# In-projection weights, block rows, query load and mask products of a block-sparse attention kernel with a gated MLP

## The chip, the cores and the metric

The kernel runs on one core of a Trainium2 chip. The time is the device time of one execution in microseconds; the kernel before has a median of 218.33 us over 3 runs (215.74 to 220.37). A profile is one further execution, recorded instruction by instruction. Its engines: PE (matmuls and transposes; PEld are its weight loads), DVE (vector), ACT (activations), POOL (GpSimd), SP (here only the issue of DMAs; SPq in the profile).

## The reference

Four sequences of 768 positions, 8 heads of 64. Attention is limited to blocks of 32 positions: the neighbours, the first and last block row and column, and three sampled blocks for each row of blocks. The result goes through a gated MLP whose gate mixes positions.

```python
scores = scale * np.matmul(q, k.transpose(0, 1, 3, 2))
mask = np.abs(blk_i - blk_j) <= window
mask = mask | (blk_i == 0) | (blk_j == 0) | (blk_i == n_blocks - 1) | (blk_j == n_blocks - 1)
for qb in range(n_blocks):
    for kb in sampled_blocks[qb]:
        mask[qb * block:(qb + 1) * block, kb * block:(kb + 1) * block] = True
scores = np.where(mask, scores, -1000000000.0)
...
attn = attn / (np.sum(attn, axis=-1, keepdims=True) + 1e-09)
x = matmul(attn, v)                       # heads side by side: 768 x 512
h = np.maximum(x @ w_in, 0.0)             # 512 x 1024
u, v = h[..., :512], h[..., 512:]
v_n = (v - mu) / np.sqrt(var + 1e-06)
v_s = np.einsum('ts,bsd->btd', w_spatial, v_n) + b_spatial[None, :, None]
out = (u * v_s) @ w_out
```

## The kernel before

**The mask inside the product.** The tile `kq` has 88 rows (`KR`): rows 0 to 63 hold the transposed keys and queries of a head (keys in columns `K_`, queries behind them; `qcols(t, n)` are the n query thirds of 256 columns from third t), rows 64 to 87 (`MR`) hold the mask. In the key columns they are a one-hot row of the block that a key belongs to; in the query columns they are -300 for each block that the query may not see, and 0 elsewhere. So one matmul over 88 rows gives scores with the mask added. The table `bm` (24 blocks x 24 blocks) is worked out on DVE from iotas and from `samp`, the sampled blocks; `mask_rows` (L293) multiplies it with the one-hot rows on PE and copies the product of one query third into the rows `MR` of head 0. `rows` (L249) copies those rows from head 0 to other heads.

**The first sequence** is done in units (`UNITS`), each of two heads by a third of the queries (pair 0: one head by two thirds), with three slots per unit, 36 slots in all. In each slot `qk_unit` multiplies queries with keys into a PSUM tile (`ps`, tag sc, two of them), and ACT takes the exponential (L438, 128 x 1024). Three to five slots later `av_unit` multiplies with the values, and DVE normalises (L461, L462). Slots 0 to 5 are pair 0, slots 6 to 14 the first query third of pairs 1 to 3, slots 15 to 23 the second third, slots 24 to 35 the last third of all pairs. From slot 36 on come whole heads (`qk_full`, L450) of the other three sequences, 144 slots.

**What feeds it.** Keys, queries and values are loaded in fp32 by SP (`load`), cast to bf16 by POOL (`cast`; the first keys by ACT), transposed by PE against an identity into a PSUM bank, and copied into `kq` by DVE. `head` and `split0` do this for pair 0 in parts, `second` and `third` (at slots 0 and 1) its further keys and its second head, `tr_first` (slots 4, 7, 9) the keys and first queries of pairs 1 to 3, `tr_rest` (slots 13, 16, 19, and 21 for pair 0) the other queries. A dictionary `at` lists what is emitted at each slot (`when`), `late` what comes after the value products; the order of each engine's instructions is the order in which the program emits them, with no scheduler. `filler` (L184) multiplies a zero tile on PE.

**The MLP of the first sequence** starts in between: `open_first` (slot 15) and the steps at slots 16, 18 and 20 multiply the first results with the v half of `w_in`; `close_first` (slot 20) deals the rest over nine slots. Its PSUM banks (`moeA`, `moeB`) are those that `bank` gives to transposes, in turn; while the first product is open, its bank is held, and transposes take the other. `w_in` comes as eight loads of 128 x 512 fp32 on SP (`w_in_load`) and eight casts on POOL (`w_in_cast`), interleaved by hand with the remaining loads and casts (L328 to L356). The weights share the six buffers of tag osb.

**The issue of DMAs.** SP issues in order, and each issue waits, besides its data and buffers, for the transfer eight before it. `samp` is the first on SP, then the queries of head 0. The first keys are issued by ACT.

Of the kernel before, what the change touches and what calls it, by code (L numbers as in the profile page):

```python
# [17 lines left out]
def _listify(ap: bass.AP) -> bass.AP:  # L18
    t = ap.tensor
    if isinstance(t.shape, tuple):  # L20
        t = dataclasses.replace(t, shape=list(t.shape))
        ap = dataclasses.replace(ap, tensor=t)
    return ap
# [3 lines left out]
def kernel(  # L27
# [39 lines left out]
    FILL, FILL2, FILL3 = 24, (2, 0, 3), 4  # L67
# [37 lines left out]
    def load(p, nm, hs=BOTH, cs=ALLC, eng=nc.sync):  # L105
        if (nm, p) not in st:
            st[nm, p] = work.tile([128, 2, S // 2], FP32, tag="st_" + nm,
                                   bufs=4 if nm == "q" else 3, name="st_" + nm)
        eng.dma_start(out=st[nm, p][:, hs, cs.start * D:cs.stop * D],
                      in_=dram(SRC[nm], p, hs, cs))  # L110
# [30 lines left out]
    load(0, "k", H0, C45, eng=nc.scalar)  # L141
    nc.sync.dma_start(out=samp[MR], in_=_listify(sampled_blocks).bitcast(I32))
    load(0, "q", H0, C03)
# [23 lines left out]
    nc.vector.memset(kq[0:D, 0, 0:TW], 0.0)  # L167
# [16 lines left out]
    def filler(n, to):  # L184
        for _ in range(n):
            nc.tensor.matmul(out=to[:, 0:128], lhsT=warm, rhs=warm, start=True, stop=True)  # L186
# [45 lines left out]
    def w_load(key, src):  # L232
        wst[key] = work.tile([128, DM], FP32, tag="osb", bufs=6, name="w_f")
        nc.sync.dma_start(out=wst[key], in_=src)

    def w_in_load(u, g):
        w_load((u, g), moe_w_in[g * 128:(g + 1) * 128, 0 if u else DH:DH if u else DFF])

    def w_in_cast(u, g, eng):
        eng.tensor_copy(out=w_in_t[:, g, 0 if u else DH:DH if u else DFF], in_=wst.pop((u, g)))  # L240
# [52 lines left out]
    def mask_rows(ps, t0, n, copy):  # L293
        nc.tensor.matmul(out=ps[:, 0:n * TW], lhsT=bm,
                         rhs=kq[:, 0, t0 * TW:(t0 + n) * TW], start=True, stop=True)
        return lambda: copy(kq[MR, 0, qcols(t0, n)], ps[0:NB, 0:n * TW])
# [15 lines left out]
    mask_rows(psum.tile([128, 1024], FP32, tag="sc", bufs=2, name="mq"), 0, 1, act_copy)()  # L312
    split0(ps0, 0, *K4, 0)
    split0(ps0, 0, *K4, 1, act_copy)
    filler(FILL2[0], wps)
# [3 lines left out]
    filler(FILL2[1], wps)  # L319
    m1 = mask_rows(psum.tile([128, 512], FP32, tag=moe_tag(), bufs=1, name="mq"), 1, 1, act_copy)  # L320
    filler(FILL2[2], wps)
    split0(psq, 0, *Q4, 1)
    m1()
    rows(H1, qcols(0, 2))
# [5 lines left out]
    cast(1, "v", PL)  # L330
    cast(2, "v", PL)
    cast(1, "q", PL, cs=C25)
    w_in_load(0, 0)
    load(3, "v")
    w_in_load(0, 1)
    load(2, "q", cs=C25)
    w_in_load(0, 2)
    w_in_load(0, 3)
    load(3, "q", cs=C25)
    w_in_load(1, 0)  # L340
    w_in_load(1, 1)
    load(0, "q", cs=C45)
    w_in_cast(0, 0, PL)
    cast(3, "v", PL)
    w_in_cast(0, 1, PL)
    cast(2, "q", PL, cs=C25)
    w_in_cast(0, 2, PL)
    w_in_cast(0, 3, PL)
    cast(3, "q", PL, cs=C25)
    w_in_load(1, 2)  # L350
    w_in_cast(1, 0, PL)
    w_in_load(1, 3)
    w_in_cast(1, 1, PL)
    cast(0, "q", PL, cs=C45)
    w_in_cast(1, 2, PL)
    w_in_cast(1, 3, PL)  # L356
# [14 lines left out]

    def mask_last():
        mask_rows(psum.tile([128, 512], FP32, tag=moe_tag(), bufs=1, name="mq"), 2, 1, dve_copy)()
# [341 lines left out]
    def c(f, *a, **kw):  # L715
        return lambda: f(*a, **kw)

    ROWS = [(2, 3, 4, K_), (2, 2, 4, qcols(0)), (4, 4, 6, K_), (5, 4, 6, qcols(0)), (8, 6, 8, K_),
            (8, 6, 8, qcols(0)), (13, 4, 8, qcols(1)), (13, 2, 4, qcols(1, 2)), (17, 4, 8, qcols(2)),
# [3 lines left out]
    when(1, c(rows, slice(2, 3), K_))  # L723
# [5 lines left out]
    when(10, mask_last)  # L729
    for p, sl in ((1, 13), (2, 16), (3, 19), (0, 21)):  # L730
        when(sl, c(tr_rest, p, 2 if p == 0 else 1))
# [142 lines left out]
```

## Time and profile before

| | |
|---|---|
| median of the runs | 218.33 us (215.74 to 220.37) |
| the profiled execution | 217.66 us |
| its span, first to last instruction | 215.6 us |
| granted TensorE clock, mean | 1.000 |
| PE busy | 201.8 us (94%) |
| ACT busy | 170.0 us (79%) |
| DVE busy | 137.1 us (64%) |
| POOL busy | 70.4 us (33%) |

The span lies within the device time of the same execution; the 2.06 us between them are outside the recorded instructions. By stretches of that execution:

```profile
0.00:20.00 20.00, 16.59 (x221) 13.97 (x222) 16.88 (x49) 16.05 (x20) 14.34 (x37) 1.00 0.92 306
20.00:40.00 20.00, 16.85 (x239) 13.55 (x240) 14.86 (x40) 16.17 (x17) 15.48 (x19) 1.00 1.11 316
40.00:60.00 20.00, 18.10 (x210) 12.01 (x211) 17.51 (x35) 17.62 (x23) 8.92 (x12) 1.00 1.04 261
60.00:80.00 20.00, 19.82 (x224) 12.34 (x224) 10.30 (x19) 18.77 (x26) 9.35 (x13) 1.00 0.83 188
```

Each line is a stretch of the span in us, its length, then the busy time and number of instructions on PE, PEld, DVE, ACT and POOL, the granted clock, the busy share of the 16 DMA engines and the GB/s that they moved. In the first 40 us PE, DVE, ACT and the DMA engines are all busy for most of the time; later PE is busy all the time. A line of the timeline shows start, busy time, engine, source line, operation, output<-input, the form, the number of instructions merged, and in brackets the idle time before them with what ended it.

### The profile page before, as it was taken

To read this page: it belongs to the slowest core of one execution; us is meant where nothing else is said; L and a number is where in the kernel's file an instruction comes from. 1 tells how busy PE (TensorE), PEld (TensorE's weight loads), DVE (VectorE), ACT (ScalarE), POOL (GpSimd) and SP (SyncE) were. 2 spreads that over 40 slices of the span, in tenths; PEclk is the share of its full clock that TensorE was granted. 3 is DMA by queue.
4 is the path that set the end of the run, shared out by engine and by line. 5 is a ranking of instruction groups with operands and counts; after the bars stand their busy time and mean duration, and the time that the engine had idled before them with its cause. 6 is when DMAs were issued, how large, how long until landed. Compare 5 with 4: busy or idle time off the path is not lost.

```text
span 215.6 us, 5244 instructions
## 1 busy us (share of the span) xinstructions
PE 201.8 (94%) x2107; PEld 127.8 (59%) x2142; DVE 137.1 (64%) x295; ACT 170.0 (79%) x225; POOL 70.4 (33%) x108
## 2 busy tenths in 40 slices
PE   7887869979999999999999999999999999999993
PEld 6676757755656666666565655656565656544441
DVE  6899686897765626367697527367694523567542
ACT  5989769979999999988999878878999878257021
POOL 5787776916194135031606004040201000004000
PEclk9999999999999999999999999999999999999999
DMA  5999999999992999999892299698010233720257
GB/s 152 349 370 369 351 360 294 154 296 293 246 290 39 245 193 311 279 220 345 111 265 52 51 272 147 166 306 235 14 22 3 51 62 75 226 105 0 45 114 280
DMA packets 64139, 41.82 MB, mean 194 GB/s; under 512 B 45172, under 2 KB 58868, under 8 KB 64116
## 3 DMA queue, kind: packets, MB, share of 16 engines
q1 hardware_dynamic: 63684, 41.17, 72.3%
q8 instruction: 16, 0.26, 0.6%
q10 hardware_dynamic: 432, 0.33, 0.5%
q14 instruction: 7, 0.06, 0.1%
HBM read 24.38 MB, written 6.29 MB: 142 GB/s over the span
## 4 chain that ended last, share of the span: by engine, by line
PE 82%; DVE 11%; ACT 4%; issue 2%; ACTq 0%
PE ps_moe L571 29%; PE ps L446 21%; PE ps_av L497 12%; PE ps_t L571 7%; PE ps L433 4%; DVE kq L224 4%; PE ps_sc L571 3%; PE ps_av L479 2%; DVE kq L254 2%; ACT a_all L450 2%; DVE vn L192 2%; PE wps L186 1%; ACT a_all L438 1%; DVE xn L462 1%; PE ps L288 1%
## 5 line engine op out<-in xcount | busy, mean ns | idle before, releaser
L450 ACT ACTIVATE a_all<-ps 128x768 bf16<-128x768 f32 x144 | 113.8, 813 | 14.4 <-PE ps L446 7.4
L446 PE MATMUL ps<-kq 88*128 88x384 bf16 x288 | 70.4, 325 | 0.7 <-ACT a_all L450 0.3
L497 PEld LDWEIGHTS <-a_all 128*128 128x128 bf16 x864 | 45.2, 97 | 20.0
L497 PE MATMUL ps_av<-vv,a_all 128*128 128x65 bf16 x864 | 49.8, 193 | 0.0
L446 PEld LDWEIGHTS <-kq 88*128 88x128 bf16 x288 | 28.0, 97 | 31.4 <-issue 1.3
L571 PE MATMUL ps_moe<-w_in_t,xt 128*128 128x512 bf16 x127 | 39.5, 378 | 1.4 <-DVE rc L461 0.7
L438 ACT ACTIVATE a_all<-ps 128x1024 bf16<-128x1024 f32 x36 | 35.3, 1028 | 6.6 <-PE ps L433 6.3
L571 PE MATMUL ps_moe<-vn,w_spt 128*128 128x512 bf16 x97 | 30.1, 378 | 0.4
L137 POOL CAST nat<-st_k 128x768 bf16<-128x768 f32 (+2 forms) x17 | 13.5, 795 | 43.2 <-DMA st_k<-in_k_dram 43.2
L608 POOL TENSOR_SCALAR std<-mv 128x3 f32<-128x3 f32 (+1 forms) x9 | 2.1, 239 | 73.3 <-DVE mv L605 51.3
L433 PE MATMUL ps<-kq 88*128 88x256 bf16 (+1 forms) x140 | 21.5, 275 | 2.2 <-DVE kq L224 1.7
L461 DVE RECIPROCAL rc<-ps_av 128x6 f32<-128x6 f32 (+1 forms) x36 | 6.6, 183 | 26.7 <-PE ps_av L497 26.6
L639 DVE SCALAR_TENSOR_TENSOR un<-ps_moe,b_col,un 128x512 bf16<-128x512 f32 x18 | 13.5, 749 | 15.5 <-PE ps_moe L571 13.3
L571 PE MATMUL ps_moe<-w_out_t,gt 128*128 128x512 bf16 x67 | 20.4, 378 | 0.3
L571 PEld LDWEIGHTS <-xt 128*128 128x128 bf16 x192 | 15.5, 98 | 8.0 <-DVE xt L224 0.8
L462 DVE TENSOR_TENSOR xn<-ps_av,rc 128x384 bf16<-128x384 f32 (+1 forms) x36 | 18.5, 513 | 1.2
L604 DVE BATCH_NORM_STATS2 stats<-vn 128x6 f32<-128x512 bf16 x24 | 16.5, 687 | 1.4 <-ACT vn L599 0.9
L224 DVE COPY kq<-tt 64x1536 bf16<-64x1536 bf16 x24 | 17.1, 712 | 0.3
L137 POOL CAST nat<-st_q 128x768 bf16<-128x768 f32 (+2 forms) x21 | 15.3, 729 | 5.4 <-DMA st_q<-in_q_dram 5.2
L479 PE MATMUL ps_av<-vv,a_all 128*128 128x65 bf16 x288 | 14.3, 193 | 2.5 <-DVE xt L224 1.9
L433 PEld LDWEIGHTS <-kq 88*128 88x128 bf16 x140 | 12.5, 97 | 6.2 <-DVE kq L224 2.3
L479 PEld LDWEIGHTS <-a_all 128*128 128x128 bf16 x288 | 13.2, 97 | 4.6 <-issue 1.8
(80 smaller groups left out, 208.3 us busy)
## 6 DMA issues: line engine op xcount, KB each, us to landing
st_v<-in_v_dram SPq DMA_DIRECT2D x16, 384.0 KB, 5.4
out_dram<-osb SPq DMA_DIRECT2D x23, 256.0 KB, 3.2
st_k<-in_k_dram SPq DMA_DIRECT2D x15, 384.0 KB, 4.5
st_q<-in_q_dram SPq DMA_DIRECT2D x12, 384.0 KB, 5.0
ws_f<-in_moe_w_spatial_dram SPq DMA_DIRECT2D x6, 384.0 KB, 6.8
w_f<-in_moe_w_in_dram SPq DMA_DIRECT2D x8, 256.0 KB, 7.0
w_f<-in_moe_w_out_dram SPq DMA_DIRECT2D x4, 256.0 KB, 4.3
st_q<-in_q_dram SPq DMA_DIRECT2D x6, 128.0 KB, 4.4
```

Of the source, the lines that this page charges most:

```text
L137: eng.tensor_copy(out=dst, in_=src)
L224: nc.vector.tensor_copy(out=o, in_=i)
L433: nc.tensor.matmul(out=ps[:, at:at + n * TW], lhsT=kq[:, h, ci * 128:(ci + 1) * 128], rhs=kq[:, h, qcols(t0, n)], start=True, stop=True)
L438: nc.scalar.activation(out=out, in_=ps, func=AF.Exp, scale=0.125)
L446: nc.tensor.matmul(out=ps[:, hf * 512:hf * 512 + HALF], lhsT=kq[:, j % H, ci * 128:(ci + 1) * 128], rhs=kq[:, j % H, S + hf * HALF:S + (hf ...
L450: nc.scalar.activation(out=a_ref["h", j][:, ci, :].rearrange("p (b c) -> p b c", b=2), in_=ps.rearrange("p (b c) -> p b c", b=2)[:, :, 0:H ...
L462: nc.vector.tensor_tensor(out=out, in0=ps[:, :, 0:D], in1=rc[:, 0:n].to_broadcast([128, n, D]), op=ALU.mult)
L479: nc.tensor.matmul(out=av_ref[u][:, to, 0:VA], lhsT=a_ref[u][:, at:at + 128], rhs=vv[pp % NVV][:, h, ci, 0:VA], start=(ci == 0), stop=(ci ...
L497: nc.tensor.matmul(out=av_ref[j][:, qc, 0:VA], lhsT=a_ref["h", j][:, ci, qc * 128:(qc + 1) * 128], rhs=vv[p % NVV][:, h, ci, 0:VA], start= ...
L571: nc.tensor.matmul(out=ref["ps"][:, 0:w], lhsT=lhs(i), rhs=rhs(i), start=(i == 0), stop=(i == n - 1))
L604: nc.vector.bn_stats(out=stats, in_=self.vn[:, tcc, :])
L639: nc.vector.scalar_tensor_tensor(out=self.un[:, tcc, :], in0=ps, scalar=b_col[:, tcc:tcc + 1], in1=self.un[:, tcc, :], op0=ALU.add, op1=AL ...
```

## The change

Four edits, with the slots and orders that go with them:

- `w_in` is fetched by two DMAs issued by POOL, each of 128 x 4 x 512 elements, which cast from fp32 to bf16 on the way. The first (v half) stands in POOL's order between the casts of the values of pairs 1 and 2, the second (u half) behind the cast of the values of pair 3. The eight loads on SP and the eight casts on POOL go.
- The mask rows of heads 2 to 7 in the second and third query thirds are written by one DMA on SP from head 0 (24 x 6 x 512 bf16), behind the last load of queries. Three row copies on DVE (slots 13, 13 and 17) go. All three mask products now come before slot 0; the third's copy was at slot 10. The row copies of heads 2 and 3 in the key columns (two of 24 x 768) become one of 24 x 1536 before slot 0.
- SP issues the first queries ahead of `samp`.
- The mask product multiplies the 24 rows `MR` only, and not all 88 with zeros in `bm`; the memset of `kq` that it needed goes.

The transposes of `tr_rest` move from slots 13, 16, 19, 21 to 12, 14, 17, 18. Between the first transposes and slot 0 PE runs four filler products in place of five.

```diff
-    FILL, FILL2, FILL3 = 24, (2, 0, 3), 4
+    FILL, FILL2, FILL3 = 24, 4, 4
...
+    load(0, "q", H0, C03)
     nc.sync.dma_start(out=samp[MR], in_=_listify(sampled_blocks).bitcast(I32))
-    load(0, "q", H0, C03)
...
-    nc.vector.memset(kq[0:D, 0, 0:TW], 0.0)
...
-    def w_in_load(u, g):
-        w_load((u, g), moe_w_in[g * 128:(g + 1) * 128, 0 if u else DH:DH if u else DFF])
-
-    def w_in_cast(u, g, eng):
-        eng.tensor_copy(out=w_in_t[:, g, 0 if u else DH:DH if u else DFF], in_=wst.pop((u, g)))
+    def w_in_load(u):
+        cs = slice(0, DH) if u else slice(DH, DFF)
+        nc.gpsimd.dma_start(out=w_in_t[:, :, cs],
+                            in_=moe_w_in.rearrange("(g p) f -> p g f", p=128)[:, :, cs])
...
-        nc.tensor.matmul(out=ps[:, 0:n * TW], lhsT=bm,
-                         rhs=kq[:, 0, t0 * TW:(t0 + n) * TW], start=True, stop=True)
+        nc.tensor.matmul(out=ps[:, 0:n * TW], lhsT=bm[MR],
+                         rhs=kq[MR, 0, t0 * TW:(t0 + n) * TW], start=True, stop=True)
...
     head(ps0, 0, *K4)
-    mask_rows(psum.tile([128, 1024], FP32, tag="sc", bufs=2, name="mq"), 0, 1, act_copy)()
     split0(ps0, 0, *K4, 0)
     split0(ps0, 0, *K4, 1, act_copy)
-    filler(FILL2[0], wps)
     psq = bank("psq", "av")
     head(psq, 0, *Q4)
     split0(psq, 0, *Q4, 0)
-    filler(FILL2[1], wps)
-    m1 = mask_rows(psum.tile([128, 512], FP32, tag=moe_tag(), bufs=1, name="mq"), 1, 1, act_copy)
-    filler(FILL2[2], wps)
+    m0 = mask_rows(psum.tile([128, 1024], FP32, tag="sc", bufs=2, name="mq"), 0, 1, act_copy)
+    mq = psum.tile([128, 1024], FP32, tag="sc", bufs=2, name="mq")
+    m1 = mask_rows(mq, 1, 1, act_copy)
+    m2 = mask_rows(mq[:, 512:1024], 2, 1, dve_copy)
+    filler(FILL2, wps)
+    m0()
     split0(psq, 0, *Q4, 1)
+    m2()
     m1()
+    rows(slice(2, 4), K_)
     rows(H1, qcols(0, 2))
...
     cast(1, "v", PL)
+    w_in_load(0)
     cast(2, "v", PL)
     cast(1, "q", PL, cs=C25)
-    w_in_load(0, 0)
     load(3, "v")
-    w_in_load(0, 1)
     load(2, "q", cs=C25)
...
     cast(3, "v", PL)
-    w_in_cast(0, 1, PL)
+    w_in_load(1)
     cast(2, "q", PL, cs=C25)
...
     cast(0, "q", PL, cs=C45)
-    w_in_cast(1, 2, PL)
-    w_in_cast(1, 3, PL)
+    nc.sync.dma_start(out=kq[MR, 2:H, qcols(1, 2)],
+                      in_=kq[MR, 0:1, qcols(1, 2)].to_broadcast([NB, H - 2, 2 * TW]))
...
-    def mask_last():
-        mask_rows(psum.tile([128, 512], FP32, tag=moe_tag(), bufs=1, name="mq"), 2, 1, dve_copy)()
...
-    ROWS = [(2, 3, 4, K_), (2, 2, 4, qcols(0)), (4, 4, 6, K_), (5, 4, 6, qcols(0)), (8, 6, 8, K_),
-            (8, 6, 8, qcols(0)), (13, 4, 8, qcols(1)), (13, 2, 4, qcols(1, 2)), (17, 4, 8, qcols(2)),
+    ROWS = [(2, 2, 4, qcols(0)), (4, 4, 6, K_), (5, 4, 6, qcols(0)), (8, 6, 8, K_), (8, 6, 8, qcols(0)),
             (20, 1, 2, qcols(2))]
-    when(1, c(rows, slice(2, 3), K_))
...
-    when(10, mask_last)
-    for p, sl in ((1, 13), (2, 16), (3, 19), (0, 21)):
+    for p, sl in ((1, 12), (2, 14), (3, 17), (0, 18)):
         when(sl, c(tr_rest, p, 2 if p == 0 else 1))
```

More of the change, by code (lines that the diff above doesn't have):

```diff
@@ L330 @@
     cast(1, "v", PL)
+    w_in_load(0)
     cast(2, "v", PL)
     cast(1, "q", PL, cs=C25)
-    w_in_load(0, 0)
     load(3, "v")
-    w_in_load(0, 1)
     load(2, "q", cs=C25)
-    w_in_load(0, 2)
-    w_in_load(0, 3)
     load(3, "q", cs=C25)
-    w_in_load(1, 0)
-    w_in_load(1, 1)
     load(0, "q", cs=C45)
-    w_in_cast(0, 0, PL)
     cast(3, "v", PL)
-    w_in_cast(0, 1, PL)
+    w_in_load(1)
     cast(2, "q", PL, cs=C25)
-    w_in_cast(0, 2, PL)
-    w_in_cast(0, 3, PL)
     cast(3, "q", PL, cs=C25)
[L350 to L353, printed above, removed]
     cast(0, "q", PL, cs=C45)
-    w_in_cast(1, 2, PL)
-    w_in_cast(1, 3, PL)
+    nc.sync.dma_start(out=kq[MR, 2:H, qcols(1, 2)],
+                      in_=kq[MR, 0:1, qcols(1, 2)].to_broadcast([NB, H - 2, 2 * TW]))
     nc.sync.dma_start(out=b_col, in_=moe_b_spatial.rearrange("(p c) -> p c", c=NCH))
```

## The prediction

> **What bounds the kernel now.** I read the page first, then the waits of the first 50 us, then the timeline of the first 30. One execution: span 215.6 us, 2.06 us around it, 217.66 in all; that is 0.67 under the median of the runs shown, 218.33. PE is busy 201.8 us (94%), and the granted clock is 1.000. From 80 to 110 us it is busy 29.6 of 30; the change touches only what comes before 45. So I ask where the first 45 us stand still.
>
> ```profile
> ACT a_all L438 <- PE ps L433: 6.3, 11, 1.4
> PE ps_av L479 <- DVE xt L224: 1.9, 2, 1.4
> PE ps L433 <- DVE kq L224: 1.7, 3, 0.8
> ```
>
> These are waits of 0 to 50 us (total, times, longest one). ACT runs 36 exponentials there, one per slot, about 1.02 us each; it is the pace, and it waits 6.3 us for scores, which wait for copies on DVE. Where:
>
> ```profile
> 14.88 1.02 ACT L438 ACTIVATE a_all<-ps 128x1024 bf16<-128x1024 f32 x1 [0.60 <-PE ps L433]
> ...
> 16.19 4.13 ACT L438 ACTIVATE a_all<-ps 128x1024 bf16<-128x1024 f32 x4 [0.28 <-PE ps L433]
> ...
> 19.42 1.58 DVE L254 COPY kq<-kq 24x1024 bf16<-24x1024 bf16 x2
> ...
> 21.03 0.88 DVE L224 COPY kq<-ps 64x512 bf16<-64x512 bf16 x2
> ...
> 21.50 0.61 PE L433 MATMUL ps<-kq 88*128 88x256 bf16 x4 [0.76 <-DVE kq L224]
> ...
> 22.21 1.02 ACT L438 ACTIVATE a_all<-ps 128x1024 bf16<-128x1024 f32 x1 [0.65 <-PE ps L433]
> ```
>
> The timeline (start, busy, engine, what, idle before). Slots 10 to 13 run from 16.19. Then the block rows of later thirds hold DVE for 1.58 us, the copies that slot 15 needs start only at 21.03, and slot 15 is late. The same timeline a little later:
>
> ```profile
> 28.88 1.03 DVE L254 COPY kq<-kq 24x256 bf16<-24x256 bf16 x1
> ...
> 29.52 1.02 ACT L438 ACTIVATE a_all<-ps 128x1024 bf16<-128x1024 f32 x1 [0.79 <-PE ps L433]
> ...
> 30.69 0.27 PE L301 MATMUL ps<-ident,nat 128*128 128x128 bf16 x2 [1.02 <-DVE vn L192]
> ...
> 31.87 11.04 ACT L438 ACTIVATE a_all<-ps 128x1024 bf16<-128x1024 f32 x11 [1.33 <-PE ps L433]
> ```
>
> Pair 0's last transposes (slot 21) wait 1.02 us for a PSUM bank that DVE empties, and slot 22 is late. From slot 14 (20.53) to slot 22 ACT stands 0.22+0.65+0.49+0.21+0.79+1.33 = 3.69 us. That is all this change can win there. After 31.87 ACT runs eleven slots without a gap, and the stop of 1.38 us behind them is untouched, so what slot 22 gains, the end gains.
>
> **The start.** Queries first: one issue on SP takes 0.37 to 0.43 us, so the query lands that much earlier (POOL waited 1.06 us for it, to 3.82) and the table that much later. DVE took the table at 2.86 without a wait, so the mask (bm, done 3.62) is late by 0 to 0.42. That bounds it: the first score needs bm, the DVE row copy behind it (0.34), the K copy (0.28), ACT's K copy, which waits for DVE's (4.49 to 4.87 now), then the mask copy on ACT (0.37), which before ran ahead of it: 5.27 to 5.63 instead of 4.87. The early query has no use. ACT's second mask copy now waits for the third on DVE (0.42, behind the two query copies of 0.61): it ends at 5.87 to 6.24. First exponential 5.95 to 6.31 instead of 5.83. The rows of heads 2 and 3 (0.93 for such a shape, 24x1536) move ahead of the copies for slots 2 and 3; by the same rows those come to 7.2 to 7.6 and 8.2 to 8.6, about when ACT asks for them. Loss 0.1 to 0.5, **0.3 taken**: bm half late. Mask products with 24 rows stream the same 256 columns: 0.27 to 0.34 each before, cost 0 to 0.3 for three, hidden beside DVE's copies; uncovered, 0.3. The memset that goes (0.17) ran while DVE waited for POOL's iota: nothing. Fillers: four against five, 0.1 each, in PE's idle time.
>
> **Slots 5 to 12.** DVE is nearly full (4.81 of 5 us at 10 to 15). Its work there is the same, so the 0.3 is carried along. The third mask's copy (0.42 at 18.30) ran while DVE waited for PE's next 8 products: nothing won there.
>
> **Slots 12 to 22, on the old clock.** From rows: scores 0.43 on PE and ready after 0.60; 8 value products 0.25; four transposes 0.25; an in-projection product 0.21; pair copies 0.88; normalisation 0.60; xt 0.28 or 0.42. Value products still wait for xn until 18.42. The transposes of pair 1's rest now follow at once, so slot 13's scores come at 18.95, not 18.66 (exp 19.55, 0.27 lost). DVE normalises to 19.38 and, with the 1.58 gone, copies 19.42 to 20.30 (21.03 to 21.91 before). Slot 14's exp 20.60; pair 2's transposes at 20.65; slot 15's scores 20.90, exp 21.62 (22.21 before). Slot 16: 22.64 (23.73). Slot 17: 23.66 (24.96). A new wait: pair 0's transposes, now in slot 18, use the bank that pair 3's filled in slot 17. PE stands from 24.50 until DVE has copied (25.15); behind it queue an in-projection product and slot 19's scores, for which ACT waits 0.55: exp 26.25. Then 27.27, 28.29, and slot 22 at 29.31 against 31.87: **2.56 won** of 3.69. The row copy of 0.51 at 25.97 is gone too, from time in which DVE would wait.
>
> **What takes the work over.** The eight HBM loads of w_in leave SP's queue and eight casts leave POOL (613 to 849 ns each), all off the path. Two casting DMAs go on POOL, the first behind the cast that ends at 13.53; the block rows go on SP behind the last query load. PE now waits for both in its own order: for the rows at slot 15 (21.2 with the 0.3), for w_in's first half at the product behind it (21.9). The DMA engines are full:
>
> ```profile
> 10.00:15.00 5.00, 4.14 (x71) 3.54 (x69) 4.81 (x9) 4.40 (x6) 4.46 (x7) 1.00 1.08 367
> 15.00:20.00 5.00, 4.45 (x85) 4.01 (x82) 4.74 (x10) 4.57 (x5) 3.59 (x6) 1.00 1.06 373
> ```
>
> Columns: window, length, busy PE, weight loads, DVE, ACT, POOL, clock, DMA share, GB/s. What had landed before by 20.77 (the cast of pair 3's queries starts without a wait) contains every byte needed at slot 15 but the last query piece (0.13 MB) and the rows (0.15 MB): 0.28/0.37 = 0.76 us more, 21.5 if the pipe only works through bytes. If later loads (SP now reaches pair 4's sooner) get in between, up to 22.5. So rows and weights land 0 to 1.3 late; near the lower end, since by 20.77 part of two further w_in pieces (issued at 14.46) had moved as well: **0.3 taken**.
> The page "DMA: Bandwidth & Descriptors" of the Trainium skill (section "Queues, rings and completion order") says each DMA engine takes turns between the queues that have work. By that, w_in's 1.05 MB from 14.5 at half of 370 GB/s would be moved by 20.2, an estimate that leaves the 0.3 as it is; no run here shows two such queues.
>
> How long POOL is held by such an issue isn't in the trace. From below 0.4 (SP's copies), from above 3.3 (SP's slowest, two transposes in 6.65). Behind the second issue queues the cast of pair 2's queries, to be done by 20.95: 13.55, two issues, two value casts of 0.83, two query casts of 0.61, so 2.2 us an issue is just in time. I take 1 us, no stall, since a copy is nearer to SP's copies; at 3.3 it is 2.2 late. Behind the row DMA on SP stand only b_col and pair 4's loads, wanted later.
>
> **Sum:** 2.56 - 0.3 - 0.3 = 2.0 won: 215.7 for this execution, 216.3 for the median.
>
> **Rivals.**
> *Weights late (slower).* PE stands at slot 15's first in-projection product, with all scores behind it. If they land after 24.2 (21.9 and the 2.3 won otherwise) the change loses, 1 us per us. Bounds: 1.05 MB at 370 GB/s lands at 16.4; four pieces in series at w_f's median of 7.0 us land at 41.5. If POOL has work to do for the transfer while DVE copies, each may hold the other up: POOL's cast of 0.83 took 1.01 beside row copies at 8.52, and DVE's 24x256 copy 1.03 beside POOL's cast at 28.27 (24x512 took 0.28 alone). DVE is over 90% busy there, so at a fifth of the rate (74 GB/s, 14 us) they land at 29, 4.8 slower: 223. Against: the collisions seen cost 0.2 to 0.8 each. Chance 0.20.
> "SBUF — State Buffer" of the Trainium skill ("Who interferes with whom") states this as a rule against the change: GpSimd can't write descriptors while VectorE holds their shared port pair, so such DMAs belong on the other issuing engines. The 1.03 and 1.01 agree with a shared port; that DMAs starve by it no run here shows.
> *POOL's issue is long*: 3.3 us each, pair 2's transposes 2.2 late, the gain gone: 218.5. Against: only SP's transposes take that. 0.13.
> *The stalls don't go.* DVE's time is freed, but POOL's casts (ws_b, 3.04 at 28.27) hold its copies as they hold that of 1.03, and the new wait at slot 18 grows by 2: 218.3, the change doing nothing. 0.10.
> *ACT without a gap*: the wait at slot 18 doesn't come, DMAs are in time: 3.69 - 0.3 = 3.4 won, 214.9. 0.17.
> *Forecast*: 0.40.
>
> **Numbers.** 216.3. The range goes from 213.5 (the gapless case less 1.4 of scatter between runs) to 221.8 (weights landing at 27.7, a rate of a quarter); outside lie 0.05 below and 0.15 above, most of the late weights. The shown runs lie 1% either side of their median, so 2% (4.4 us) is about what can be told from no change. Below 213.96: less than half of the gapless case and the edge of the forecast, 0.13. Above 222.7: 0.14, the late weights but for those of a quarter of the rate and more. Within: 0.73.
>
> **What would show it.** Exp of slot 0 at 5.95 to 6.31; no row copies on DVE from 16.5 to 26; slot 15's scores at 21.2 and slot 22's exp at 29.6; a wait of PE for DVE at 24.8. Wrong if PE's first product with w_in waits for its DMA beyond 22, or if pair 2's queries are cast after 20.95.

## The result, and the profile after

The changed kernel takes 217.82 us (median of 20 runs, 216.76 to 220.38); the kernel before, timed beside it, 216.66 us (20 runs, 214.39 to 220.37). The ratio is 1.0087, with a 95% interval from 1.0063 to 1.0112: slower by 0.9%, where 2.0 us less were forecast. Here and below a ratio leaves out the runs that lie more than 1.5% above the fastest of their kernel, and a median leaves out none, so the two need not agree. The profiled execution of the changed kernel took 217.28 us, with a span of 215.2. That is less than the 217.66 of the profile of before, which lay a whole microsecond above its median, so the two spans can't be compared; their stages can.

The page first: the chain of waits that ended last, as shares of the span.

```profile
PE 81%; DMA 10%; DVE 3%; ACT 3%; SPq 1%; POOL 1%; issue 1%; ACTq 0%
PE ps_moe L557 31%; PE ps L432 21%; PE ps_av L483 12%; PE ps_t L557 7%; DMA w_in_t<-in_moe_w_in_dram 5%; PE ps_sc L557 3%; DMA st_v<-in_v_dram 3%; PE ps L419 3%; PE ps_av L465 2%; ACT a_all L436 2%; DMA st_k<-in_k_dram 2%; DVE vn L191 1%; SPq L109 1%; DVE kq L223 1%; POOL vv L137 1%
```

A DMA of `w_in` holds 5% of the span. The same chain in order of time (start, length, what) shows what leads to it:

```profile
6.95 6.21 DMA st_v<-in_v_dram
13.22 1.09 POOL vv L137
14.31 10.93 DMA w_in_t<-in_moe_w_in_dram
```

The values of pair 1 land at 13.2, POOL casts them, POOL issues the first casting DMA at 14.31, and it lands 10.93 us later, at 25.24. Everything after hangs on that. No exponential of slots 0 to 14 is in this stretch of the chain: it doesn't matter here how early they ran. The timeline of ACT (columns as before), against the lines of before that end in 0.65, 0.79 and 1.33:

```profile
7.18 1.98 ACT L424 ACTIVATE a_all<-ps 128x1024 bf16<-128x1024 f32 x2 [0.54 <-PE ps L419]
...
17.84 3.03 ACT L424 ACTIVATE a_all<-ps 128x1024 bf16<-128x1024 f32 x3 [0.28 <-PE ps L419]
21.74 3.01 ACT L424 ACTIVATE a_all<-ps 128x1024 bf16<-128x1024 f32 x3 [0.86 <-PE ps L419]
26.13 3.00 ACT L424 ACTIVATE a_all<-ps 128x1024 bf16<-128x1024 f32 x3 [1.39 <-PE ps L419]
29.90 17.26 ACT L424 ACTIVATE a_all<-ps 128x1024 bf16<-128x1024 f32 x17 [0.77 <-PE ps L419]
```

And the timeline of PE behind the last two waits:

```profile
25.28 0.38 PE L557 MATMUL ps_moe<-w_in_t,xt 128*128 128x512 bf16 x1 [1.41 <-DMA w_in_t<-in_moe_w_in_dram]
...
28.94 0.27 PE L299 MATMUL ps<-ident,nat 128*128 128x128 bf16 x2 [0.68 <-DVE kq L223]
```

The stalls of before are gone: slots 13 to 15 run without a gap, and from slot 19 on ACT runs 17 slots in a row. In their place stand a wait of 0.86 us at slot 13 (0.27 forecast), a wait of 1.4 us for the weights at slot 16, the forecast wait for a bank at slot 19 (0.68 on PE, 0.77 on ACT), and a first exponential at 7.18 in place of 5.83. ACT's waits for scores in the first 50 us fall from 6.3 to 4.6 us; most of what is lost at the start isn't counted among them. Slot 22 starts at 32.92; before it was 31.87, the forecast was 29.6.

The window from 15 to 20 us, on which the forecast of the DMAs rested, and the next one, now with 263 and 270 GB/s where before they had 373 and 346 (two lines of after, then the second window of before):

```profile
15.00:20.00 5.00, 4.09 (x73) 3.40 (x71) 4.84 (x8) 4.26 (x6) 4.86 (x8) 1.00 1.15 263
20.00:25.00 5.00, 3.23 (x58) 3.02 (x59) 3.79 (x12) 3.89 (x4) 1.56 (x2) 1.00 1.17 270
```

```profile
20.00:25.00 5.00, 3.68 (x57) 2.93 (x55) 3.76 (x10) 3.43 (x5) 4.13 (x7) 1.00 1.04 346
```

The DMA share, in which the times of packets are added up, is still above 1: the engines were not idle. The profile counts a packet of the casting DMA by what it writes (1 KB of bf16), and it reads twice that.

### The profile page after: what moved, and what is told of

It is laid out like the page before. It is cut to its first block, busy times and chain, and to the rows that moved or that the text cites. A ratio compares the mean times of both kernels' runs of the same rounds, so it can differ in the third digit from the quotient of the medians.

```text
span 215.2 us, 5258 instructions
## 1 busy us (share of the span) xinstructions
PE 205.5 (95%) x2141; PEld 128.6 (60%) x2141; DVE 131.7 (61%) x290; ACT 170.4 (79%) x225; POOL 66.8 (31%) x102
## 3 DMA queue, kind: packets, MB, share of 16 engines
q0 software_dynamic: 1056, 1.05, 2.9%
## 4 chain that ended last, share of the span: by engine, by line
PE 81%; DMA 10%; DVE 3%; ACT 3%; SPq 1%; POOL 1%; issue 1%; ACTq 0%
PE ps_moe L557 31%; PE ps L432 21%; PE ps_av L483 12%; PE ps_t L557 7%; DMA w_in_t<-in_moe_w_in_dram 5%; PE ps_sc L557 3%; DMA st_v<-in_v_dram 3%; PE ps L419 3%; PE ps_av L465 2%; ACT a_all L436 2%; DMA st_k<-in_k_dram 2%; DVE vn L191 1%; SPq L109 1%; DVE kq L223 1%; POOL vv L137 1%
## 5 line engine op out<-in xcount | busy, mean ns | idle before, releaser
L483 PEld LDWEIGHTS <-a_all 128*128 128x128 bf16 x864 | 45.2, 97 | 20.0
L432 PEld LDWEIGHTS <-kq 88*128 88x128 bf16 x288 | 28.0, 97 | 31.4 <-issue 1.3
L557 PE MATMUL ps_moe<-w_in_t,xt 128*128 128x512 bf16 x144 | 44.0, 378 | 1.4 <-DMA w_in_t<-in_moe_w_in_dram 1.4
L557 PE MATMUL ps_moe<-vn,w_spt 128*128 128x512 bf16 x108 | 32.7, 377 | 0.0
L419 PE MATMUL ps<-kq 88*128 88x256 bf16 (+1 forms) x140 | 22.9, 287 | 1.1 <-DVE kq L223 0.7
L557 PE MATMUL ps_moe<-w_out_t,gt 128*128 128x512 bf16 x72 | 21.5, 378 | 0.0
L419 PEld LDWEIGHTS <-kq 88*128 88x128 bf16 x140 | 13.0, 100 | 6.7 <-issue 2.3
L137 POOL CAST nat<-st_q 128x768 bf16<-128x768 f32 (+2 forms) x21 | 14.6, 698 | 6.2 <-DMA st_q<-in_q_dram 6.2
L137 POOL CAST vv<-st_v 128x768 bf16<-128x768 f32 x16 | 14.3, 893 | 4.5 <-DMA st_v<-in_v_dram 4.0
L465 PE MATMUL ps_av<-vv,a_all 128*128 128x65 bf16 x288 | 14.3, 193 | 1.1 <-DVE rc L447 0.9
L191 DVE TENSOR_SCALAR vn<-vn,mv,rstd 128x512 bf16<-128x512 bf16 x24 | 13.4, 592 | 2.9 <-POOL rstd L596 2.9
```

The costliest lines, as they stand in the source:

```text
L137: eng.tensor_copy(out=dst, in_=src)
L191: nc.vector.tensor_scalar(out=out, in0=in0, scalar1=s1, scalar2=s2, op0=o0, **kw)
L419: nc.tensor.matmul(out=ps[:, at:at + n * TW], lhsT=kq[:, h, ci * 128:(ci + 1) * 128], rhs=kq[:, h, qcols(t0, n)], start=True, stop=True)
L432: nc.tensor.matmul(out=ps[:, hf * 512:hf * 512 + HALF], lhsT=kq[:, j % H, ci * 128:(ci + 1) * 128], rhs=kq[:, j % H, S + hf * HALF:S + (hf ...
L465: nc.tensor.matmul(out=av_ref[u][:, to, 0:VA], lhsT=a_ref[u][:, at:at + 128], rhs=vv[pp % NVV][:, h, ci, 0:VA], start=(ci == 0), stop=(ci ...
L483: nc.tensor.matmul(out=av_ref[j][:, qc, 0:VA], lhsT=a_ref["h", j][:, ci, qc * 128:(qc + 1) * 128], rhs=vv[p % NVV][:, h, ci, 0:VA], start= ...
```

## The experiments

Sixteen runs. A variant keeps the changed kernel ("after") or the kernel before as its base and differs by the edit shown. The table has what is read from each for what follows: ratio to before with its interval, median, the time from which the trace's clock record shows the full PE clock, and the start of the exponentials of slots 0, 13 and 22 and of the first one of slot 36 (stage 2). The medians of before, timed beside them, were 216.3 to 216.8. Ahead of the time of the full clock the record has no entry, and the views print 1.00; the products of PE show it: the four of a slot's scores take 1.01 to 1.06 us before it and 0.60 after.

| run | ratio (95%) | median us | full clock | slot 0 | 13 | 22 | 36 |
|---|---|---|---|---|---|---|---|
| before, first profile | | 216.66 | 3.84 | 5.83 | 19.29 | 31.87 | 47.39 |
| after | 1.0087 (1.0063 to 1.0112) | 217.82 | 9.84 | 7.18 | 21.74 | 32.92 | 47.05 |
| u1 after, table first | 1.0091 (1.0041 to 1.0141) | 218.14 | 11.73 | 7.20 | 23.00 | 32.62 | 46.42 |
| u2 after, w_in as before | 0.9977 (0.9934 to 1.0019) | 215.91 | 12.79 | 7.06 | 21.80 | 31.41 | 45.22 |
| u3 after, rows on DVE | 1.0099 (1.0047 to 1.0151) | 219.71 | 13.02 | 7.45 | 23.14 | 34.39 | 49.87 |
| u4 after, 32 fillers | 1.0114 (1.0059 to 1.0168) | 219.97 | 6.38 | 6.86 | 20.60 | 32.30 | 46.85 |
| b0 before, second profile | | 216.28 (one) | 5.41 | 6.10 | 19.34 | 31.93 | 46.04 |
| f1 before + casting DMAs | 1.0143 (1.0087 to 1.0199) | 218.54 | 9.96 | 6.59 | 22.08 | 33.04 | 48.51 |
| f2 before + queries first | 1.0169 (1.0120 to 1.0219) | 219.35 | 9.80 | 7.57 | 21.45 | 34.44 | 49.91 |
| c2 u2 + 32 fillers | 0.9952 (0.9922 to 0.9983) | 214.56 | 4.06 | 6.82 | 19.86 | 29.48 | 43.40 |
| f3 before + rows, slots | 0.9990 (0.9947 to 1.0033) | 215.33 | 12.34 | 6.86 | 21.66 | 31.27 | 45.22 |
| c3 c2, table first | 0.9974 (0.9938 to 1.0010) | 214.92 | 5.73 | 6.62 | 19.79 | 29.47 | 43.68 |
| d1 after, w_in 3 us earlier | 1.0107 (1.0038 to 1.0176) | 217.03 | 12.38 | 7.36 | 22.08 | 31.70 | 46.63 |
| d2 after, w_in in pieces | 0.9991 (0.9942 to 1.0039) | 215.97 | 4.83 | 6.70 | 20.30 | 29.92 | 43.72 |
| e1 before, 32 fillers | 1.0033 (0.9997 to 1.0069) | 217.07 | 4.22 | 6.47 | 19.85 | 31.70 | 47.17 |
| e2 f2 + 32 fillers | 1.0086 (1.0044 to 1.0127) | 217.87 | 5.46 | 6.88 | 19.79 | 31.74 | 45.86 |
| e3 d2 + 32 fillers | 0.9985 (0.9947 to 1.0022) | 215.51 | 6.17 | 6.77 | 19.75 | 29.66 | 43.47 |
| e5 e3, one piece at 2.8 | 0.9969 (0.9936 to 1.0002) | 215.18 | 4.64 | 6.80 | 20.30 | 30.53 | 44.33 |

From slot 36 to the end all of them take 168.0 to 169.7 us. A profile is one execution: single columns scatter, above all where POOL and DVE meet.

### Taking one part out of the changed kernel

u1: the table ahead of the queries again.

```diff
-    load(0, "q", H0, C03)
     nc.sync.dma_start(out=samp[MR], ...)
+    load(0, "q", H0, C03)
```

> Only the table's load goes back ahead of the first queries. Theory A (the start is the loss): the table lands before 3, bm is done at 3.6 to 3.8, the first exponential comes at 6.0 to 6.4 instead of 7.18 and PE runs its matmuls at the short length (0.60 for four of 256 columns) from about 4; 0.8 to 1.2 us won, ratio to before about 1.003 to 1.005. Rival B (the weights' landing sets the time, whatever comes before): the first exponential comes as early, but the wait of PE for w_in grows from 1.41 to 2.2 or more, it ends at 25 as now, and the time stays within 0.3 us of the change's (ratio 1.007 to 1.011).

The table came in time (the comparison with it starts at 2.87, not 3.93; the first keys' cast at 3.04, not 3.44), yet slot 0 stayed at 7.20 and the time at 1.009. PE's products had the longer time until 11.7 us, and slot 22 is within 0.3 us of after. The time is the one that rival B gives, the way to it isn't: the profile has no wait for `w_in`, since a stop of 1.51 us at slot 9 had come first, where row copies on DVE stood beside POOL's work. So within this kernel the place of the table isn't what the time hangs on.

u2: the eight loads and eight casts of `w_in` as before. The row DMA stands behind pair 2's second load of queries and not behind the last one; it is issued at 12.03 us (12.18 in after).

```diff
-    w_in_load(0)
...
+    w_in_load(0, 0)
+    load(3, "v")
+    w_in_load(0, 1)
...
+    w_in_cast(0, 0, PL)
```

> Only the weights go back to eight loads on SP and eight casts on POOL; the row DMA stands on SP behind pair 2's second query load. Theory B (the weights' landing sets the time): no wait of PE for w_in, slot 16's exponential comes at 24.5 to 25.0 instead of 26.13, 1.2 to 1.5 us won, ratio 0.998 to 1.003. Theory A (the start alone): first exponential still near 7.2, ratio 1.006 to 1.010.

1.0087 becomes 0.9977, the largest step of any single edit on after, and no wait for `w_in` on PE is left. Slot 0 is as late as in after (7.06): the way of the weights, not the start, makes the loss against before.

u3: the block rows by the DVE copies of slots 13 and 17, in place of the row DMA.

```diff
-    nc.sync.dma_start(out=kq[MR, 2:H, qcols(1, 2)], ...)
+    (13, 4, 8, qcols(1)), (13, 2, 4, qcols(1, 2)), (17, 4, 8, qcols(2)),
```

> Only the block rows of the later thirds go back to DVE, at slots 13 and 17; the transposes keep their early slots. If the row DMA is what the change wins: slower than the change by 1 to 2 us (ratio 1.013 to 1.018). If the wait for the weights hides it: DVE's 1.58 at slot 13 falls into that wait, and the time is the change's within 0.4 us (ratio 1.007 to 1.011).

The ratio can't be told from that of after; its runs scatter most of all (216.1 to 224.0), and the profile is of one of 220.42. Inconclusive. In after, the scores of slot 15 did not wait for the row DMA.

u4: 32 fillers in place of 24 at the start.

```diff
-    FILL, FILL2, FILL3 = 24, 4, 4
+    FILL, FILL2, FILL3 = 32, 4, 4
```

> 32 products of a zero tile on PE before the first transposes instead of 24, about 0.9 us more. If the half length of PE's matmuls until 9.8 comes from PE standing between 3.7 and 5.5: matmuls at the short length from 4 to 7 on, slot 3's exponential 0.3 to 0.8 earlier; if the weights' landing sets the time, the end stays (ratio 1.007 to 1.011), else 0.3 to 0.8 us are won (1.004 to 1.007).

The full clock came at 6.4, the first nine slots ran without a gap, and the time did not fall. The timeline of PE shows why:

```profile
24.66 0.38 PE L557 MATMUL ps_moe<-w_in_t,xt 128*128 128x512 bf16 x1 [1.93 <-DMA w_in_t<-in_moe_w_in_dram]
```

Slot 13 is 1.14 us earlier, and PE waits 1.93 us instead of 1.41: the wait for the weights takes about half of what the start wins. 0.62 are still there at slot 22 and 0.20 at slot 36; what the fillers cost at the end of the kernel is told below, with e1 and e2.

### A second look at before, and one part of the change alone

b0: the kernel before, unchanged.

> The kernel before, unchanged, profiled a second time. Its first profile (217.66 us) lies 1.4 above the median of the 35 timed runs, 216.26, and the profile of the changed kernel (217.28) 0.5 below its own, 217.82: the two profiles say 0.4 faster, the timed runs 1.9 slower. If the stalls of the first 45 us are the same in every execution (theory 1), this one starts its first exponential at 5.8, has the stop of about 1.4 near 45.5 and stage 2 from 47.4. If some of them come by chance (theory 2: collisions of DVE and POOL in the copies for stage 2), the stop near 45.5 is gone or shorter, stage 2 starts at 45.5 to 46.5 and the span is 213 to 214.5.

Theory 2. The stalls up to slot 22 are the same (31.93), and the stop of 1.38 us near 45 isn't there. It stands in the profiles of before, u3, f1, f2 and e1 (1.33 to 1.49), and in no other of the 18. So it doesn't belong to every execution of before, and it is more than the microsecond by which the first profile lies above the median. All five that have it make the row copies of slots 13 and 17 on DVE; b0 and e2 make them too and don't have it; of the eleven with the row DMA none has it. So the change may well take it away, though no run was made to show that.

f1: the casting DMAs alone, on before.

```diff
-    w_in_load(0, 0)
...
-    w_in_cast(0, 0, PL)
...
+    w_in_load(0)
...
+    w_in_load(1)
```

> The kernel before with the casting DMAs alone (two on POOL in place of eight HBM loads on SP and eight casts on POOL); start, row copies and slots as before. Taking them out of the changed kernel won 1.1% (1.0087 to 0.9977). Theory A (weights late: the first half lands 11 to 14 us after its issue, since the casting queue moves slowly beside the loads): the product with w_in in slot 15 waits for it to about 24 to 25, though slot 15 itself is 1 us later in this kernel, so that 0.5 to 2 of the wait show: 1.004 to 1.011, and a wait of PE for w_in in the first 30 us. Theory B (the loss is in the combination, because slots 12 to 18 come earlier there): no wait for w_in here, 0.998 to 1.003.

Its time lies above the range of theory A, which the interval reaches, and its profile has no wait for `w_in`, as theory B has it: neither fits. It has a late clock (with the very start of before), the stop near 46, and this (timelines of DVE and of ACT):

```profile
12.59 2.75 DVE L253 COPY kq<-kq 24x1536 bf16<-24x1536 bf16 x2
...
17.37 1.02 ACT L423 ACTIVATE a_all<-ps 128x1024 bf16<-128x1024 f32 x1 [1.50 <-PE ps L418]
```

Two row copies take 2.75 us; in before the same pair takes 1.29 and 1.58, in f3, where POOL happened to rest, 0.75. In f1 they stand beside a cast, the issue of the DMA and a cast on POOL without a pause. So the loss of 1.4% is measured, and where it goes in the median execution isn't settled.

f2: the queries ahead of the table alone, on before.

```diff
+    load(0, "q", H0, C03)
     nc.sync.dma_start(out=samp[MR], ...)
-    load(0, "q", H0, C03)
```

> The kernel before with the first query load ahead of the sampled table, nothing else. Theory A (the later table delays the mask, PE stands between its fillers and the first products and misses the early clock): full clock only after 9 us, first exponential at 6.8 to 7.2 in place of 5.83, and 1.002 to 1.006. Theory B (what makes the changed start slow is the new order of the mask products and fillers, as the run with the table first suggests): the mask is 0.4 late at most, first exponential 5.9 to 6.3, 0.999 to 1.003.

1.7%, more than any theory had for it. The table was late by 1.04 us (its comparison at 3.90, before 2.86), not by the 0.41 of one issue, and the first keys' cast by 0.58 (3.61). PE stood from 3.7 to 4.1, and its products had the longer time until 9.8; slot 0 at 7.57.

f3: the remaining parts on before: row DMA, early slots, products of 24 rows, the third mask product at the start.

```diff
-        nc.tensor.matmul(out=ps[:, 0:n * TW], lhsT=bm,
...
+        nc.tensor.matmul(out=ps[:, 0:n * TW], lhsT=bm[MR],
...
+    mask_rows(...  2, 1, dve_copy)()
...
+    nc.sync.dma_start(out=kq[MR, 2:H, qcols(1, 2)], ...)
...
-    for p, sl in ((1, 13), (2, 16), (3, 19), (0, 21)):
+    for p, sl in ((1, 12), (2, 14), (3, 17), (0, 18)):
```

> The kernel before with the rest of the change alone: mask products of 24 rows, the third mask product at the start in place of slot 10, the block rows of later thirds by one DMA on SP, and the transposes of pairs' rest at slots 12, 14, 17 and 18. The load order of the start and the weights' way are as before. Theory A (the prediction's main term holds: 2.56 us of stalls go between slots 12 and 22): slot 22 at about 29.6 with the first exponential at 6, and a time of 0.986 to 0.991. Theory B (the bank wait of slot 18 and POOL's casts take it over): 0.993 to 1.001. If A, the three edits alone sum to about 1.4 + 1.7 - 1.1 = 2.0% loss, while together they make 0.9%: then the two losses overlap (a late start hides part of the wait for the weights).

The stretch from slot 13 to slot 22 fell from 12.6 us to 9.6, as the prediction had it (9.8). But the clock came at 12.3 in this profile, slot 0 was 1.0 us late and slot 13 2.4, and the ratio is 0.999, in the range of theory B.

### The start

c2: u2 with 32 fillers. c3: that, and the table ahead of the queries (the edits of u4 and u1).

```diff
-    FILL, FILL2, FILL3 = 24, 4, 4
+    FILL, FILL2, FILL3 = 32, 4, 4
```

> The changed kernel with w_in loaded and cast as before (0.9977, first exponential 7.06) and with 32 filling products at the start in place of 24, which brought the full clock to 6.4 us where w_in was late. If the time is set by what lands last and that is not w_in any more (theory A), an earlier start is carried through to stage 2: first exponential 6.6 to 6.9, nine slots without a gap, 0.992 to 0.997. If something else takes the gain over (theory B: the bank wait of slot 18, later query loads), the same 0.9977 within 0.002.

> The changed kernel with w_in loaded and cast as before, 32 filling products, and the sampled table ahead of the first query again. With 32 fillers alone it was 0.9952 (first exponential 6.82, waiting for the mask). Theory A (the table's place costs what the queries-first kernel showed, up to 1.7%): first exponential 6.0 to 6.5, 0.985 to 0.993. Theory B (that loss came mainly from the missed clock, which the fillers mend): 0.993 to 0.997.

c2 is faster than both kernels: 214.56 us (214.34 to 215.12, the least scatter of all), ratio 0.9952, interval below 1. Its timeline of ACT:

```profile
6.82 9.56 ACT L439 ACTIVATE a_all<-ps 128x1024 bf16<-128x1024 f32 x10
16.66 2.87 ACT L439 ACTIVATE a_all<-ps 128x1024 bf16<-128x1024 f32 x3 [0.28 <-PE ps L434]
19.86 5.82 ACT L439 ACTIVATE a_all<-ps 128x1024 bf16<-128x1024 f32 x6 [0.34 <-PE ps L434]
26.45 6.01 ACT L439 ACTIVATE a_all<-ps 128x1024 bf16<-128x1024 f32 x6 [0.77 <-PE ps L434]
```

The one gap of size left before slot 24 is the 0.77 of the bank. With the weights out of the way the eight fillers seem to win (0.9977 to 0.9952; the intervals overlap, so this isn't clear of the noise), where in u4 they won nothing. c3 isn't different from c2: theory B there.

e1 and e2: 32 fillers on before, and on f2.

```diff
-    FILL, FILL2, FILL3 = 24, (2, 0, 3), 4
+    FILL, FILL2, FILL3 = 32, (2, 0, 3), 4
```

> The kernel before with 32 filling products in place of 24, nothing else. Theory A (its scatter from 214.1 to 219 is the clock that comes early in some executions and late in others): full clock before 6.5 us, the spread shrinks, and the median falls by 0.5 to 1, to 0.995 to 1.000. Theory B (the eight fillers only delay the first transposes by 0.5, and the scatter comes from later collisions): spread as before, 1.000 to 1.004.

> The kernel before with the first query load ahead of the table and 32 fillers. Theory A (the loss of 1.7% with 24 fillers was mostly the missed clock): full clock before 6.5, first exponential 6.3 to 6.9, 0.998 to 1.005. Theory B (the late table itself, through the order of the copies and PE's queue): 1.010 to 1.017 as with 24 fillers.

On before, whose clock was early in both profiles anyway, the fillers cost 0.5 us at slot 0 and gain nothing. With queries first they take the loss from 1.0169 to 1.0086; the intervals just touch. So about half of what the order of the loads costs there goes with the clock; 0.5% against e1 remain for the late table itself, with intervals that overlap.

The fillers have a price at the other end of the kernel as well. In all seven profiles with 32 of them the last eight products wait 0.59 to 0.83 us for the last transposed `gt` (PE of c2, at the end of its span):

```profile
207.38 0.61 PE L572 MATMUL ps_sc<-w_out_t,gt 128*128 128x256 bf16 x4 [0.69 <-DMA gt<-un]
```

None of the eleven with 24 fillers has this wait; from slot 36 to the end they take 168.0 to 168.7 us, the seven 169.0 to 169.7. In the seven a packet of 16 KB on the queue q8 (instruction) starts 1.8 to 2.0 us after the issue of that transpose, in the eleven none starts within 8 us of it. So eight more products at the start may shift a load of instructions into that transfer; that it is what holds it was not tried.

### The weights

The packets on the DMA engines in the changed kernel, by queue (packets, MB, share of 16 engines), from 14.3, the issue, to 18.2, then from 18.3 to 21.0, then to 25.1; q0 is POOL's queue, q1 is SP's:

```profile
q1 hardware_dynamic: 1289, 1.10, 109.4%
...
q0 software_dynamic: 422, 0.43, 95.3%
q1 hardware_dynamic: 183, 0.22, 25.2%
...
q0 software_dynamic: 425, 0.42, 60.4%
q1 hardware_dynamic: 468, 0.70, 53.7%
```

For 3.97 us after the issue no packet of q0 moves. Then the two casting DMAs, 512 packets each, take most of the engines for 3 us, and share them with SP's loads from 21 on: keys, queries and values of the next pair, and gate weights, which now are issued 4 to 6 us earlier than before (keys at 14.25, before 20.02) and are wanted later than `w_in`. By 22.07 the 512th packet has started, but the first DMA counts as landed at 25.24. Besides its 512, each casting DMA has sixteen packets of 4 bytes in the trace. Fifteen of them have started by 22.63 and the sixteenth starts at 24.92: read as the ends of sixteen parts, one part alone made the last 2.3 us.

d1: the first casting DMA ahead of the casts of pair 3's keys, at 11.32 in place of 14.31.

```diff
+    w_in_load(0)
     cast(3, "k", PL)
     cast(3, "q", PL, cs=C01)
     cast(1, "v", PL)
-    w_in_load(0)
```

> The changed kernel with the first casting DMA issued ahead of the casts of pair 3's first part (about 11.4 us in place of 14.3). Theory A (its packets first move about 3.6 us after the issue whatever POOL does next, and then take turns with SP's loads): first packets at 15, landing at 22 to 23.5, the wait of PE for w_in gone or below 0.5, and 1.000 to 1.006; the value and query loads of that time are late by part of it. Theory B (the turns with the loads cost as much as the early issue wins): a later scores' wait for query or value casts takes its place, 1.006 to 1.011.

Its first packet moves at 15.79, 4.5 us after the issue, and PE no longer waits for it: slots 13 to 22 take 9.6 us. But POOL now waits 1.43 and 1.21 us for query pieces, the clock came late, and the interval of the ratio holds both theories' values, and that of after.

d2: each casting DMA as four of 128 rows.

```diff
-        nc.gpsimd.dma_start(out=w_in_t[:, :, cs], in_=...)
+        for g in range(4):
+            nc.gpsimd.dma_start(out=w_in_t[:, g, cs], in_=moe_w_in[g * 128:(g + 1) * 128, cs])
```

> The changed kernel with each casting DMA as four of 128 rows. If the 3.6 us from the issue to the first packet is the time in which the descriptors of a whole DMA are made (theory A), the first packets come about 1.3 to 2 us after the issue, the first half lands 1 to 2 earlier, and the time is 1.002 to 1.007; POOL is held longer in all by the eight issues. If it is a latency that every such DMA has, or DVE's hold on a port (theory B), the first packet still comes 3.3 to 4 us behind the issue, and with POOL held longer (0.7 to 1 per issue) pair 2's queries are cast 3 to 5 us later: 1.010 to 1.025.

The first packet still comes 4.4 us after the issue (theory B's delay), but the time is better than theory A's: 0.9991. Each piece lands by itself (7.2 to 10.3 us after its issue), and PE's first product with `w_in` runs at 22.27 without a wait:

```profile
22.27 0.38 PE L557 MATMUL ps_moe<-w_in_t,xt 128*128 128x512 bf16 x1
```

POOL's eight issues take 0.54 to 0.78 each and delay nothing that was wanted.

e3: that with 32 fillers. e5: that, with one piece of the second half issued at 2.83, where POOL would wait for queries and DVE for the table.

```diff
+    nc.gpsimd.dma_start(out=w_in_t[:, 3, 0:DH], in_=moe_w_in[384:512, 0:DH])
     cast(0, "k", nc.scalar, H0, C03)
     cast(0, "q", PL, H0, C03)
...
-        for g in range(4):
+        for g in range(3 if u else 4):
```

> The changed kernel with each casting DMA as four of 128 rows, and 32 fillers. With the whole casting DMAs and 32 fillers it was 1.0114. Theory A (the wait was for the end of one large DMA whose packets take turns with the loads; pieces land one by one): no wait for w_in over 0.5 us, 0.993 to 0.999. Theory B (the four-piece run gained by its early clock alone): PE waits 1 us or more for w_in, 1.003 to 1.012.

> The kernel with four pieces and 32 fillers, in which one piece of the second half is issued by POOL at about 2.8 us, where POOL waits for queries and DVE has little to do. Theory A (the delay from issue to first packet belongs to such a DMA by itself): its first packet comes 3.3 us or more after the issue, at 6 or later. Theory B (it comes from the full queues or from DVE's work): 1 to 2.5 us, at 4 to 5.3. The time within 0.3% of the kernel without it, if its 0.26 MB among the first loads costs 0 to 0.7 us at the start.

e3 has no wait for `w_in`, and with 0.9985 it is 1.3% below u4, which differs from it only by the pieces; the intervals don't overlap. In e5 the packets by queue from 2.8 to 6.1, then from 6.2 to 8.5 (q10 is ACT's queue):

```profile
q1 hardware_dynamic: 586, 0.66, 78.5%
q10 hardware_dynamic: 195, 0.10, 10.3%
...
q0 software_dynamic: 144, 0.13, 44.8%
```

The first packet of q0 moves at 6.21, 3.4 us after the issue, which is theory A's time. It doesn't exclude theory B: DVE waited for the table from 2.9 to 3.9, but was busy for 2.21 of the 3.38 us, and the DMA engines were at 0.90. What speaks against DVE is that the delay doesn't follow it: 3.3 us with DVE busy for 97% of them (u3), 4.5 with 68% (d1). In the other runs, issued between 11 and 14.4 us, it was 3.3 to 4.6.

## Why the prediction was wrong

**The step that failed** is the last of those under "what takes the work over": "rows and weights land 0 to 1.3 late ... 0.3 taken". It let the transfer begin at its issue, at 14.5, and asked only when the pipe would have worked through the bytes. Three things came late instead: the issue (14.31 against 13.55, since the values whose cast stands ahead of it landed at 13.2), the first packet (3.97 us behind it), and the end (a DMA of 1.05 MB counts when its last packet is there, and shares the engines until then). It landed at 25.2, 3 us behind the forecast. u2 against after, which takes back the whole way of the weights, prices it: 1.1%, or 2.4 us, of the 3.2 between the forecast of 2.0 won and the 1.2 lost; e3 against u4, which differ by the pieces alone, agrees (1.3%). A smaller slip stands in the range: at a quarter of 370 GB/s from 14.5 on the weights would land at 25.9, not at 27.7.

**The rival that came true** is "weights late": loss from 24.2 on, 1 us per us. At 25.2 that makes 1.0; the medians differ by 1.2. That the two meet is partly luck: d1 and u1 have no wait for `w_in` in their profiles and are as slow (1.0107 and 1.0091). Its reason isn't shown: it held DVE's copies responsible for keeping POOL from the work of the transfer, and the delay before the first packet doesn't follow DVE's share (3.3 us at 97%, 4.5 at 68%). "SBUF — State Buffer" of the Trainium skill ("Who interferes with whom") has that reason as a rule; no run here shows it at work on these DMAs. "DMA: Bandwidth & Descriptors" of the Trainium skill ("Queues, rings and completion order") has the turns between queues, and the trace agrees from 21.0 on (60.4% and 53.7% side by side); in the 2.7 us before, the shares were 95.3% and 25.2%. The estimate from it, 20.2, failed by its starting time: the first packet moved at 18.28, not at 14.5.

**The start** was taken at 0.3, bounded by 0.5, and cost 1.35 at slot 0 and more by slot 13. Two links were missing. A small table behind a larger load on the same queue came 1.07 us later, not one issue later. And the full clock came late: the same products take 1.01 in place of 0.60 (timeline of PE after, then before).

```profile
6.13 1.01 PE L419 MATMUL ps<-kq 88*128 88x256 bf16 x4
```

```profile
5.20 0.60 PE L433 MATMUL ps<-kq 88*128 88x256 bf16 x4
```

PE goes from its fillers into the transposes without a pause in before, and stands still for a moment in after. That this pause loses the early clock isn't so in every execution: d2, with the start of after and longer pauses, had the full clock at 4.83, and f1, with the start of before and no pause behind the fillers, only at 9.96 (PE of d2, then of f1).

```profile
4.21 0.39 PE L299 MATMUL ps<-ident,nat 128*128 128x128 bf16 x2 [0.49 <-ACT nat L135]
...
6.06 0.60 PE L419 MATMUL ps<-kq 88*128 88x256 bf16 x4 [0.47 <-ACT kq L226]
```

```profile
3.51 0.42 PE L300 MATMUL ps<-ident,nat 128*128 128x128 bf16 x2
...
5.49 1.06 PE L418 MATMUL ps<-kq 88*128 88x256 bf16 x4
```

With d2's early clock slot 0 comes at 6.70, so 0.87 of the 1.35 stay without the late clock (0.60 against b0), still above the bound of 0.5. In the changed kernel the start costs little by itself that the times show (u1, u4). Where the weights come as before it can cost more: f2 lost 1.7%, but c2 and c3, with 32 fillers, don't differ.

**What was right.** Slots 13 to 22: with the weights in time and the clock early they take 9.6 to 9.9 us (c2, c3, d2, e3; 10.2 in e5), against 9.8 forecast. Slot 22 then comes at 29.5 to 29.9 (30.5 in e5), against 29.61; that this meets too is partly luck, since slot 0 is 0.3 to 0.9 later there than the forecast had it, and the stop of 0.60 at slot 9 is gone there. The row DMA is hidden, the wait at slot 19 is there (0.68 on PE, forecast 0.65 from 24.50 to 25.15), an issue on POOL takes 0.98 and 0.90 (1 taken). What the 24-row products and the memset cost no run tells: f3 has the products beside a late clock.

**Half right: what slot 22 gains, the end gains.** c2 is 2.4 us ahead at slot 22 and 1.8 in the median (214.56 against 216.39), and its stretch from slot 36 to the end is 1.0 longer than in before, 0.69 of it the wait for `gt` that comes with 32 fillers. And the stop near 45 was called untouched; it isn't in every execution of before and in none with the row DMA, so the profile that the sum was made against was a long one. Taken from the median of the 20 runs, 216.66, the 2.0 forecast would have been 214.7.

**What stays open.** Where f1's 1.4% lies in its usual execution; what the clock record's late start hangs on when the program of the start is the same (before and b0 early, f1 late; d2 early, after late); what makes the 3.3 to 4.6 us before the first packet; whether the change takes away the stop near 45.

## What to carry to other kernels

A load that is moved to another queue has to be timed anew from its issue: what it queues behind on the issuing engine, when its first packet moves, with whom it shares the engines, and when its last packet is there; one transfer that feeds several products did better here in four pieces. When the chain of waits runs back through a transfer, a gain ahead of it can be lost in the wait, as in u4. One profile of before isn't the kernel: a second one would have shown that one of its stalls isn't always there. And a few products more at the start can be paid for at the end: compare the last microseconds too.

## What was not expected of the hardware

- A DMA issued by POOL, casting fp32 to bf16, moved its first packet 3.3 to 4.6 us after its issue in all nine profiles that have one, whether it had 512 or 128 rows to move, and with DVE busy for 65% of that time (e5) as for 97% (u3).
- A row copy of 24x512 on DVE takes 0.28 us alone. Beside POOL's casts it took between that and 0.94, and 1.60 where it began during the issue of a casting DMA that two casts followed (f1 and u1). Beside issues and at most 0.13 us of a cast it took 0.33 in e3 and 0.84 in e5: whether the issue holds it too isn't settled.
- With 24 fillers the full clock came at 3.8 to 5.4 us in three of the profiles and at 9.8 to 13.0 in eight; with 32 it came by 6.4 in all seven. The times of c2 scatter by 0.8 us, those of before by 6.0. The stretch at full clock is a whole number, 59 to 62, of 3.41 us in all 18 profiles, so the clock seems to change on a grid of that step, whose place differs between executions. The 24 fillers run for 2.74 us, less than a step, and the 32 for 3.59, more than one; that this is why 32 suffice was not tried apart.
